# Batch 0 in a new order: beacons by a casting DMA, one transposed piece per score group, 96-token transposes for pairs 4 to 11

## The chip, the cores and the metric

The kernel runs on one core of a Trainium2 chip. The metric is the device time of one execution in microseconds (us), lower is better. A comparison uses runs of both kernels made on the same chip in the same rounds. A run more than 1.5% above the fastest run of its kernel is called slow, and only fast runs enter a ratio. PE is the matrix engine, PEld its weight loads, DVE the vector engine, ACT the scalar engine, POOL the GpSimd engine, SP (SyncE) an engine that here only issues DMA. SPq and POOLq are the issuing sides of these engines. kT<-k_dram and the like name what is written and what is read; st is a staging buffer, sc the scores, p a pair that was cast to bf16.

## The reference

There are 8 batches of 8 heads, 576 tokens, 16 beacons and a head size of 64. Beacons are extra keys and values that stand ahead of the tokens. A feed-forward layer with a maximum of three products follows.

```python
scores = scale * np.matmul(q, concat([beacon_k, k]).T)      # causal over the tokens only
a = softmax(scores)
x = np.matmul(a, concat([beacon_v, v]))                     # -> [4608 tokens, 512]
h = np.maximum(np.maximum(x @ w1, x @ w2), x @ w3)          # 512 -> 768
out = h @ w_out                                             # 768 -> 512
```

## The kernel before

The 32 pairs of heads (four in each batch) are worked through in order. For each pair the kernel needs q and k transposed (qT and kT, three buffers of each), computes scores in four groups on PE, takes exp on ACT, and later multiplies with v on PE (PV). The feed-forward units fill PE in between. PE transposes pairs 0 to 11 (batches 0 to 2) itself. For pairs 12 to 31, POOL casts the staged data to bf16, SyncE stores it to DRAM, and a transposing DMA fetches it back into qT and kT.

Loads, stores, transposing fetches and the output stores are nearly all issued by SyncE, which takes them in order. How loads are issued:

```python
st_pool = ctx.enter_context(tc.tile_pool(name="st", bufs=9))      # staging buffers for q/k pairs and v pieces
...
loads = [L(load_pair, 0, nc.scalar), L(load_beacons, 0, B_PE, bk32_0)]   # the beacons use no staging buffer
loads += [L(load_pair, 1, nc.scalar)] + load_pairs(2, 4) + load_v_pieces(0)
loads += load_pairs(4, 8) + load_v_pieces(1)
loads += load_pairs(8, 12) + load_v_pieces(2) + [L(load_beacons, B_PE, B, bk32)]
for b in range(B_PE, B):
    loads += load_pairs(b * PPB, (b + 1) * PPB) + load_v_pieces(b)

def next_load(n=1):                   # issue the next n of the list
    for _ in range(n):
        if loads:
            loads.pop(0)()

def C(fn, *a):                        # a cast frees a staging buffer, then one more load is issued
    def run():
        fn(*a)
        next_load()
    return run

def start():
    keep_busy(14)
    next_load(10)                     # 10 entries = 9 staged loads + the beacons
    ...
```

Nine buffers and nine staged loads: at first, each later load is issued just after the cast that frees its own buffer. Here are the fetch and the store of pairs 12 to 31, and their places in the program, where `p` is the first pair of batch `b`:

```python
def store_pair(p):                    # nc.sync.dma_start, twice (L276)
def fetch_pair(p):                    # nc.sync.dma_start_transpose into qT (L283) and kT (L284)
...
    at_step(p + i - 4, 0, C(cast_pair, p + i, by_pool, by_pool))
    at_step(p + i - 3, 0, L(store_pair, p + i))
    at_step(p + i - 2, 1, L(fetch_pair, p + i))
```

Pairs 0 to 11 are loaded as 128 rows of nine tokens each (packets of 2304 bytes), transposed in 36 tiles of 64, and DVE copies both results out of PSUM. The line numbers in the profile are those of the kernel concerned. The score matmul is L361 before and L381 after; kT's two DVE copies are L309 (16 beacon columns) and L310 (576 token columns), after the change L329 and L330; the v loads are L207 and L214; the q and k loads of 96 rows are L166 and L173; the v casts on POOL are L223 and L230; the fetches are L283 and L284, after the change L291 and L292, and the stores L276, after the change L284.

The softmax here doesn't subtract the row's maximum and nothing guards it: scores larger than these inputs give would overflow.

## Time and profile before

| | before |
|---|---|
| median of 3 runs | 308.89 us (308.16 to 312.95) |
| span of the profiled execution | 304.3 us |
| PE busy | 285.4 us, 94% of the span |
| DMA, share of busy time up to 86 us (about 1 is full; the records add up to a little more) | 0.86 to 1.11 |
| first exp of pairs 0, 5, 12, 31 | 10.76, 37.84, 93.66, 238.82 us |

The profile's page of the kernel before, cut to lines of its parts 2 and 4: the span in 40 slices, each digit a busy share in tenths (PEclk is the clock granted to PE), and then the shares of the chain of work that ended last.

```profile
PE   7698789899899999999999999999999999999994
PEclk9999999999999999999999999999999999999999
DMA  7999999799999999999999999688214001103003
...
PE 86%; DVE 6%; issue 2%; ACT 2%; DMA 1%; SPq 0%; POOL 0%; POOLq 0%; DVEq 0%
```

After the first dozen slices PE is full until the last one. The table by windows of the kernel before, cut to four rows, says the same; its columns are the window, its length, the busy time of PE, PEld, DVE, ACT and POOL with the number of instructions, the granted clock, the DMA share and GB/s.

```profile
10.00:37.00 27.00, 24.09 (x502) 13.34 (x502) 16.87 (x45) 18.53 (x27) 12.98 (x21) 1.00 1.11 258
37.00:86.00 49.00, 44.27 (x689) 22.35 (x700) 32.54 (x65) 24.19 (x36) 27.55 (x56) 1.00 1.03 247
86.00:120.00 34.00, 33.63 (x471) 17.08 (x476) 19.33 (x37) 18.67 (x28) 17.96 (x36) 1.00 1.01 235
120.00:240.00 120.00, 119.00 (x1566) 64.56 (x1580) 71.50 (x136) 63.24 (x94) 57.44 (x115) 1.00 0.83 175
```

From 86 to 240 us PE is busy 99% of the time. PE idles earlier: in batch 0 and in pairs 5 to 11. The clock column needs care here: the trace holds no clock record before 24.06 us, and a matmul of 256 columns takes 0.40 us ahead of that and 0.28 us after it, so the 1.00 of the first window is only the lack of a record.

The waits of the kernel before (engine and line, the releaser, then us in total, times, longest us), cut to two lines, one for what the scores wait for and one for SyncE.

```profile
PE sc L361 <- DVE kT L310: 5.6, 6, 2.8
...
SPq L166 <- POOL v_sb L223: 1.6, 1, 1.6
```

The scores wait for DVE's copies and, once, 0.6 us for ACT; no score waits for a fetched kT. This is what SyncE does around the first fetch, that of pair 12 (timeline of SyncE before: start, duration, engine, line, operation, tiles, count). Its scores start on PE at 93.17 us.

```profile
83.68 4.21 SPq L207 DMA_DIRECT2D st<-in_v_dram  x3
87.99 1.78 SPq L283 DMA_TRANSPOSE qT<-q_dram  x1
89.83 1.24 SPq L284 DMA_TRANSPOSE kT<-k_dram  x1
...
92.21 1.18 SPq L207 DMA_DIRECT2D st<-in_v_dram  x2
```

The fetch is issued behind three v loads, and two more v loads follow it. The trace gives 92.49 us as the landing of kT, so the fetch has 0.7 us to spare. Nothing in the views of waits shows how little that is.

### The profile page before, as it was taken

The numbers are of one execution on the slowest core, as the hardware profiler recorded it, in microseconds if no ns is written. First come the engines' busy times: TensorE is split into PE (matmuls) and PEld (weight loads), VectorE is DVE, ScalarE is ACT, GpSimd is POOL, SyncE is SP. The second block draws the span as 40 slices with busy tenths as digits, with TensorE's granted clock in tenths as the row PEclk, the third lists the DMA queues.
The fourth block names the chain that finished last, engine by engine and source line by source line (L and its number), as shares of the span: only waits on it lengthen the run. The fifth ranks groups of instructions, "written<-read, shape, count | busy, mean of one in ns | idle before, by whom it ended". The sixth has DMA issues, their size and how long they took to land.

```text
span 304.3 us, 8877 instructions
## 1 busy us (share of the span) xinstructions
PE 285.4 (94%) x3673; PEld 147.7 (49%) x3710; DVE 177.3 (58%) x343; ACT 139.2 (46%) x208; POOL 122.3 (40%) x243
## 2 busy tenths in 40 slices
PE   7698789899899999999999999999999999999994
PEld 4254544445454545454545777545454554444441
DVE  1695557774766465646564656465646574284472
ACT  3467754355436354635463546354635431401300
POOL 3580673465744554455445544654243210000000
PEclk9999999999999999999999999999999999999999
DMA  7999999799999999999999999688214001103003
GB/s 251 254 317 238 248 289 211 174 243 227 309 242 187 235 287 234 184 239 295 212 195 242 281 200 208 124 182 129 55 54 125 2 2 69 72 1 137 3 0 138
DMA packets 87976, 53.96 MB, mean 177 GB/s; under 512 B 67200, under 2 KB 79488, under 8 KB 87936
## 3 DMA queue, kind: packets, MB, share of 16 engines
q1 hardware_dynamic: 86000, 49.66, 69.2%
q0 software_dynamic: 1648, 3.15, 5.5%
q8 instruction: 29, 0.48, 0.7%
q10 hardware_dynamic: 288, 0.59, 0.6%
q14 instruction: 11, 0.09, 0.1%
HBM read 35.13 MB, written 15.42 MB: 166 GB/s over the span
## 4 chain that ended last, share of the span: by engine, by line
PE 86%; DVE 6%; issue 2%; ACT 2%; DMA 1%; SPq 0%; POOL 0%; POOLq 0%; DVEq 0%
PE fps L469 41%; PE pv L423 12%; PE fps L486 12%; PE sc L361 10%; PE sc L469 5%; PE sc L486 2%; DVE qT L301 1%; DVE kT L310 1%; DMA bk<-in_beacon_k_dram 1%; PE fps L330 1%; DVE xT L446 1%; DVE hT L479 1%; ACT at_sb L370 1%; DVE kT L309 1%; PE fps L293 1%
## 5 line engine op out<-in xcount | busy, mean ns | idle before, releaser
L370 ACT ACTIVATE at_sb<-sc 128x992 bf16<-128x992 f32 (+3 forms) x128 | 103.9, 860 | 106.7 <-PE sc L361 104.2
L469 PE MATMUL fps<-xT,w_sb 128*128 128x512 bf16 (+1 forms) x622 | 136.6, 355 | 1.9 <-issue 0.8
L469 PEld LDWEIGHTS <-w_sb 128*128 128x128 bf16 x720 | 65.7, 97 | 71.0 <-issue 13.4
L386 POOL TENSOR_SCALAR_AFFINE_SELECT at_sb<-at_sb 128x256 bf16<-128x256 bf16 (+2 forms) x140 | 51.1, 384 | 114.5 <-ACT at_sb L370 114.5
L479 DVE TENSOR_TENSOR hT<-hT,fps 128x512 bf16<-128x512 bf16 x96 | 65.6, 685 | 39.0 <-PE fps L469 39.0
L361 PE MATMUL sc<-qT,kT 64*128 64x288 bf16 (+4 forms) x384 | 37.7, 294 | 6.3 <-DVE kT L310 5.6
L486 PE MATMUL fps<-w_out_sb,hT 128*128 128x512 bf16 x172 | 40.6, 379 | 1.0 <-issue 0.8
L477 DVE CAST hT<-fps 128x512 bf16<-128x512 f32 x42 | 28.9, 689 | 20.8 <-PE fps L469 20.8
L494 DVE COPY y<-fps 128x512 f32<-128x512 f32 x30 | 20.7, 688 | 27.7 <-PE fps L486 27.7
L486 PEld LDWEIGHTS <-hT 128*128 128x128 bf16 x216 | 20.4, 98 | 25.2 <-DVE hT L479 1.3
L446 DVE TENSOR_TENSOR xT<-pv,recip 128x288 bf16<-128x288 f32 (+2 forms) x96 | 28.1, 348 | 6.4 <-ACT recip L443 3.8
L180 POOL CAST p<-st 96x768 bf16<-96x768 f32 x40 | 31.8, 822 | 0.0
L361 PEld LDWEIGHTS <-kT 64*128 64x128 bf16 x384 | 13.6, 95 | 33.6 <-issue 22.9
L423 PE MATMUL pv<-at_sb,v_sb 128*32 128x96 bf16 (+8 forms) x1408 | 29.4, 230 | 0.0
L423 PEld LDWEIGHTS <-v_sb 128*32 128x32 bf16 (+1 forms) x1408 | 24.4, 97 | 2.2 <-issue 0.9
L223 POOL CAST v_sb<-st 128x1536 bf16<-128x1536 f32 (+2 forms) x24 | 21.1, 894 | 2.8 <-DMA st<-in_v_dram 2.8
L423 PE MATMUL pv<-at_sb,ones 128*32 128x288 bf16 (+4 forms) x512 | 17.5, 258 | 1.6 <-DVE xT L446 1.5
L469 PE MATMUL sc<-xT,w_sb 128*128 128x512 bf16 x71 | 18.3, 380 | 0.1
L441 ACT ACTIVATE lnd<-pv 128x288 f32<-128x288 f32 x32 | 13.2, 413 | 8.0 <-PE pv L423 7.3
L479 DVE TENSOR_TENSOR hT<-hT,sc 128x512 bf16<-128x512 bf16 x12 | 8.2, 687 | 12.5 <-PE sc L469 6.8
L423 PEld LDWEIGHTS <-ones 128*32 128x32 bf16 (+1 forms) x512 | 10.9, 96 | 8.1 <-DVE xT L446 2.6
L443 ACT ACTIVATE recip<-lnd 128x288 f32<-128x288 f32 x32 | 14.2, 443 | 1.0
(38 smaller groups left out, 108.2 us busy)
## 6 DMA issues: line engine op xcount, KB each, us to landing
st<-in_q_dram SPq DMA_DIRECT2D x32, 288.0 KB, 5.0
out_dram<-y SPq DMA_DIRECT2D x36, 256.0 KB, 3.6
st<-in_k_dram SPq DMA_DIRECT2D x30, 288.0 KB, 5.3
st<-in_v_dram SPq DMA_DIRECT2D x24, 256.0 KB, 5.6
q_dram<-p SPq DMA_DIRECT2D x20, 144.0 KB, 2.2
k_dram<-p SPq DMA_DIRECT2D x20, 144.0 KB, 2.3
w_sb<-in_moe_w_dram POOLq DMA_DIRECT2D x6, 384.0 KB, 8.4
st<-in_v_dram SPq DMA_DIRECT2D x8, 224.0 KB, 5.6
```

What stands on the lines that cost most here:

```text
L180: cast(t16.rearrange("p r h d -> p h r d"), st[0:QP, i * NQ2 : (i + 1) * NQ2].rearrange("p (h r d) -> p h r d", h=2, r=QR),)
L223: cast(v_sb[0:n, t:t1].rearrange("p t h d -> p (t h d)"), st[0:n, (t - t_lo) * H * D : (t1 - t_lo) * H * D],)
L361: nc.tensor.matmul(ps[:, e, off : off + q1 - q0], kT[hs, 128 * t : 128 * t + 128], qT[hs, q0:q1], start=True, stop=True, tile_position=(64 ...
L370: nc.scalar.activation(out=both_heads(p, gi), in_=ps[:, :, 0 : g_width[gi]], func=AF.Exp, scale=scale)
L386: nc.gpsimd.affine_select(out=view, in_=view, compare_op=ALU.is_ge, fill=0.0, base=x0, pattern=[[0, 2], [1, hi - lo]], channel_multiplier=-1,)
L423: nc.tensor.matmul(ps[32 * j : 32 * j + 32, bank, lo + q0 - qa : lo + qb - qa], lhsT, at_view(PPQ * quad + j // 2, t, j % 2, q0, qb), star ...
L446: nc.vector.tensor_mul(xT[:, 2 * g + part - 1, c0 + ca : c0 + cb], ps[:, bank, lo : lo + cb - ca], recip[:, ca:cb],)
L469: nc.tensor.matmul(ps[:, o0 : o0 + n], w_in[i][:, ct, 128 * ft : 128 * (ft + 1)], xT[:, ct, x0 : x0 + n], start=(ct == 0), stop=(ct == n_c ...
L477: (by_act if alone[0] else by_dve)(hT[:, ft, :], ps)
L479: nc.vector.tensor_max(hT[:, ft, :], hT[:, ft, :], ps)
L486: nc.tensor.matmul(ps, hT[:, ft, 128 * tt : 128 * (tt + 1)], w_out_sb[:, ft, :], start=(ft == 0), stop=(ft == n_ft - 1),)
L494: nc.vector.tensor_copy(y, ps)
```

## The change

The intent is an earlier start and fewer waits in batch 0. The beacons come by a casting DMA from POOL, so that POOL has no cast to make. The transposes of batch 0 are spread, one piece behind each score group, instead of a whole pair behind the first. Pairs 4 to 11 are loaded as 96 rows of six tokens (packets of 1536 bytes) and turned by 12 transposes of 96 tokens; from pair 6 on ACT copies q out beside DVE, which copies k. The first weight load moves from step (1,1) to (0,3), and two feed-forward units move forward to step (4,3). The diff, cut to its core:

```diff
+    P_NINE = 4
...
+    for b in range(B_PE):
+        nc.gpsimd.dma_start(
+            out=bk16_0[Nb * b : Nb * (b + 1)], in_=beacon_k[b].rearrange("h n d -> n h d")
+        )
...
-            if b < B_PE:
+            if p < P_NINE:                       # 128 rows of 9 tokens, else 96 rows of 6
...
-    loads = [L(load_pair, 0, nc.scalar), L(load_beacons, 0, B_PE, bk32_0)]
-    loads += [L(load_pair, 1, nc.scalar)] + load_pairs(2, 4) + load_v_pieces(0)
-    loads += load_pairs(4, 8) + load_v_pieces(1)
-    loads += load_pairs(8, 12) + load_v_pieces(2) + [L(load_beacons, B_PE, B, bk32)]
-    for b in range(B_PE, B):
+    loads = [L(load_pair, 0, nc.scalar), L(load_pair, 1, nc.scalar)] + load_pairs(2, 4)
+    loads += load_v_pieces(0)
+    loads += load_pairs(4, 6) + load_v_pieces(1) + load_pairs(6, 8)
+    for b in range(2, B):
+        if b == B_PE:
+            loads.append(L(load_beacons, B_PE, B, bk32))
         loads += load_pairs(b * PPB, (b + 1) * PPB) + load_v_pieces(b)
...
     def start():
-        keep_busy(14)
+        keep_busy(13)
         next_load(10)
...
-        by_pool(bk16_0, bk32_0)
...
     def turn(p, i, ps):
         src = stage.pop(("pair16", p, i))
+        if p >= P_NINE:
+            for r in range(QR):
+                nc.tensor.transpose(ps[:, r * QP : (r + 1) * QP], ..., ident[0:QP, 0:QP])
+            return
...
-        copy(kT[:, 0:Nb], bT[:, pi, Nb * b : Nb * (b + 1)])
+        if p > 0:
+            copy(kT[:, 0:Nb], bT[:, pi, Nb * b : Nb * (b + 1)])
...
-    at_step(1, 1, L(load_w, 0, 0, d_ff))
+    at_step(0, 3, L(load_w, 0, 0, d_ff))
...
+    fine_at = {
+        (0, 0): [L(turn_apart, 1, 0)],
+        (0, 1): [L(turn_apart, 1, 1)],
+        ...
+        (2, 2): [L(turn_apart, 4, 0)],
+        (2, 3): [L(turn_apart, 4, 1)],
+        ...
+    }
...
-                    turn_pair(nxt, False)
+                    turn_pair(p + 1, by_act)
```

## The prediction

> **What bounds the kernel now.** The chain of waits is 86% PE. The table by windows splits the run: from about 86 us on PE is busy 98-99%, so only time saved before that counts, and it then counts in full. Before, there are three kinds of loss.
> (a) Start: the first scores run at 10.11 us. The chain shows why: the beacon DMA lands at 6.2, POOL casts it (0.61), PE turns it, ACT copies it, then DVE copies kT 1.69 + 0.67 us.
> (b) Batch 0 (10.1 to 37.0, where pair 5's scores start): 20 score groups whose exps cost ACT 17.3 us; PE runs slow until 24.06 us, where the trace's first full-clock record stands (a 256-column matmul takes 0.40 us before it, 0.28 after).
> (c) Pairs 5 to 10 (37 to 86 us): PE idle about 5 us in the windows, mostly 0.6-0.7 us a pair waiting for DVE's qT (0.76) and then kT (0.16 + 0.74) drain.
>
> **What the change does.**
> Start: the POOL cast and the wait of kT for the beacons vanish; first scores near 7.6 us, 2.5 earlier.
> Batch 0: the same turns, but 18 transposes between score groups; fewer keep-busy matmuls; PV a little later; two FFN units (8 matmuls of 0.215 = 1.7 us) pulled forward.
> Later turns: 12 transposes of 96 columns for 36 tiles of 64, about the same PE time (0.76 us now). ACT drains q (about 0.64) beside DVE's k, which takes some 0.5 us a pair off the wait, five or six times: about 2.5-3 us.
>
> **What gives part of it back: the DMA queue.** DMA is saturated from 6 to 36 us (share 1.0 in the windows). The weight load w0 now is issued right after pair 3's casts, at about 11.4 instead of 15.5 us, and its first packet should flow 3.6 us later as before (15.5 to 19.1), thus near 15, when the second part of v (landed 17.3 now) and pairs 4 and 5 (17.8-20.1) are still under way. The Trainium skill ("DMA: Bandwidth & Descriptors", Queues, rings and completion order) says that an engine goes round-robin between queues, packet by packet; the trace agrees: while weights flow (packets of 247 ns) beside v (256-byte packets, 18 ns), the weights' queue takes 0.93 of the DMA and v 0.15 (26 to 28 us). So v's second part should slip to about 20-21 us and pair 4 to 22-23, while pair 4's first turn stands in PE's order at group (2,2), otherwise reached near 20. PE stalls there for 2-3 us, and the start's gain is lost. From there ACT's exps and four normalisations pace the rest: pair 5's scores at 36-37.7 us, but with two FFN units done.
>
> **Sum.** Pair 5: -0.7 to +1; units +1.7; later waits +2.5 to 3; and, if pair 4 is not late, up to 3 more. About 5.7 us off 308.9.
>
> Predicted **303.2 us**, 299 to 307.5. Faster by over 2%: 0.43; within: 0.53; slower: 0.04.
>
> **What would show it.** First scores at 7.4-8 us; POOL's cast of pair 4 waiting for v or pair 4 data at 20-23 us and PE idle then; pair 5's scores near 36; waits of scores for kT in pairs 5-10 down from 0.65 to below 0.15 us; windows after 86 us unchanged in length; busy PE time about 1-2 us less.
>
> **What would make it wrong.** If w0 does not push v and pair 4 back, batch 0 ends at 33-34 and the time is about 300. If the slow PE clock lasts longer (fewer keep-busy matmuls, an idle stretch), the gain shrinks to 2-3 us. If the 96-column turns cost 1 us or more each, or ACT's added copies delay exps, (c) is lost. Run-to-run spread (308.2 to 313.0) is as large as half the effect.

## The result, and the profile after

| | before | after |
|---|---|---|
| median us (lowest to highest), 4 runs of each in the same rounds | 309.00 (308.16 to 312.95) | 329.52 (326.88 to 330.18) |
| span of the profiled execution, us | 304.3 | 327.2 |
| first exp of pair 5 | 37.84 | 37.70 |
| pair 9 | 68.67 | 64.32 |
| pair 11 | 86.52 | 86.65 |
| pair 12 | 93.66 | 100.11 |
| pair 16 | 124.09 | 137.12 |
| pair 24 | 185.05 | 208.89 |
| pair 31 | 238.82 | 262.65 |

The change makes the kernel slower: ratio 1.0658, 95% interval 1.0583 to 1.0733. All ratios here are the mean time of one kernel's fast runs over that of the other's fast runs of the same rounds, so they are not quite the ratio of the medians that stand beside them.

The table of first exps, read from the trace, is the main reading: up to pair 9 the new kernel is 4.35 us ahead, at pair 11 the lead is gone, and from pair 12 to pair 24 it falls 23.8 us behind. From there on both run alike. The page of the kernel after, the same lines:

```profile
PE   5868999986948996999699985999999999999995
PEclk9587999997996998999989997999999999999999
DMA  8999999899999399967999579826732300301103
...
PE 78%; DMA 8%; DVE 5%; SPq 4%; issue 2%; ACT 1%; POOL 0%; DVEq 0%
```

PE has holes up to slice 25, and after several of them PEclk has a dip as well. SyncE and DMA now stand in the chain, with 12% between them. The table by windows of the kernel after:

```profile
10.00:37.00 27.00, 22.23 (x441) 13.06 (x439) 17.37 (x48) 19.63 (x28) 13.17 (x18) 0.77 1.15 225
37.00:86.00 49.00, 43.11 (x545) 21.72 (x548) 32.45 (x55) 26.54 (x40) 29.68 (x58) 0.97 1.04 238
86.00:120.00 34.00, 27.31 (x357) 13.76 (x362) 14.44 (x28) 13.72 (x21) 13.49 (x28) 0.90 0.90 203
120.00:240.00 120.00, 108.49 (x1394) 59.92 (x1406) 62.88 (x119) 54.97 (x83) 54.07 (x106) 0.96 0.82 182
```

Between 86 and 240 us PE is idle 18.2 us, where it had been idle 1.4. The waits of the kernel after, cut to four lines:

```profile
PE sc L381 <- DMA kT<-k_dram: 16.8, 4, 6.0
PE sc L381 <- DVE kT L330: 5.0, 5, 3.6
PE fps L300 <- POOL p L187: 2.2, 1, 2.2
...
SPq L173 <- POOL v_sb L230: 14.3, 3, 6.1
```

Four score groups wait 16.8 us for a fetched kT; before there was no such wait. One waits 3.6 us for a DVE copy. SyncE, in turn, waits 14.3 us with a load in hand for a staging buffer that POOL's v casts free; before it was 1.6. The timeline of PE in the kernel after, cut to those four score groups (the bracket is the idle time ahead and the releaser):

```profile
99.41 0.90 PE L381 MATMUL sc<-qT,kT 64*128 64x288 bf16 x8 [6.04 <-DMA kT<-k_dram]
...
127.94 0.54 PE L381 MATMUL sc<-qT,kT 64*128 64x288 bf16 x8 [2.87 <-DMA kT<-k_dram]
...
163.16 0.90 PE L381 MATMUL sc<-qT,kT 64*128 64x288 bf16 x8 [3.15 <-DMA kT<-k_dram]
...
199.69 0.57 PE L381 MATMUL sc<-qT,kT 64*128 64x288 bf16 x8 [4.70 <-DMA kT<-k_dram]
```

They are the scores of pairs 12, 15, 19 and 23: one in each batch from 3 to 5, and two in the first of these. The timeline of SyncE in the kernel after, around the first of them and then into the second:

```profile
87.08 3.13 SPq L214 DMA_DIRECT2D st<-in_v_dram  x1
...
91.68 0.43 SPq L284 DMA_DIRECT2D q_dram<-p  x1
92.15 1.56 SPq L284 DMA_DIRECT2D k_dram<-p  x1
93.81 1.10 SPq L214 DMA_DIRECT2D st<-in_v_dram  x2
95.02 1.54 SPq L291 DMA_TRANSPOSE qT<-q_dram  x1
96.61 1.25 SPq L292 DMA_TRANSPOSE kT<-k_dram  x1
...
105.96 1.22 SPq L292 DMA_TRANSPOSE kT<-k_dram  x1
113.39 0.31 SPq L173 DMA_DIRECT2D st<-in_q_dram  x1
```

The fetch of pair 12 now stands behind all the v loads and behind two stores. It is issued 6.8 us later than before (96.61 against 89.83 for kT) and lands at 99.37 us. And between 107.2 and 113.4 us SyncE issues nothing at all: it holds the q load of pair 22, whose buffer is freed by the v cast that POOL ends at 113.36 us. The table by windows shows the DMA engines resting at a share of 0.02 from 109 to 114 us, while later fetches wait behind that load.

The clock records of the kernel after, in the trace: full speed from 29.40 to 77.19 us, then half speed at 77.19 to 80.60, 97.67 to 104.50, 128.39 to 131.80, 162.52 to 165.94 and 200.07 to 203.48. Each of these starts around the end of one of PE's long waits. The Trainium skill ("TensorE: Matmul & The Clock Gate", Part 1: The HAM clock gate) says that the clock is judged in free-running windows of 3413 ns and falls to one half after an idle one. The lengths agree: the half-speed records last 3413 ns and 6827 ns. But the window ahead of a drop need not be wholly idle: in the 3.41 us before these five drops PE was busy 0.80, 0.00, 0.54, 0.89 and 0.38 us, while every window after 30 us that full speed followed held 1.7 us or more. So a missed fetch costs its wait and then a slow stretch: after its 6.04 us of waiting, pair 12 took 9.76 us to pair 13, against 7.68 before.

The wait of 3.6 us for DVE is of another kind. The timelines of DVE and of POOL in the kernel after, around pair 10's copy of 16 beacon columns (128x16, SBUF to SBUF):

```profile
72.04 3.65 DVE L329 COPY kT<-bT 128x16 bf16<-128x16 bf16 x1
```

```profile
70.68 1.60 POOL L187 CAST p<-st 96x768 bf16<-96x768 f32 x2
72.23 0.77 POOL L406 TENSOR_SCALAR_AFFINE_SELECT at_sb<-at_sb 128x256 bf16<-128x256 bf16 x2
72.94 1.60 POOL L187 CAST p<-st 96x768 bf16<-96x768 f32 x2
74.47 1.18 POOL L230 CAST v_sb<-st 128x512 bf16<-128x512 f32 x2
```

The eight POOL instructions follow each other without a gap from 70.68 to 75.65 us. The copy, which takes 0.16 us when POOL is idle (pair 2, 15.42 us), starts inside this run, and ends 0.03 us after it.

### The profile page after: what moved, and what is told of

The parts are those of the page before. It is cut to its first block, busy times and chain, and to the rows that moved or that the text cites. A ratio compares the mean times of both kernels' runs of the same rounds, so it can differ in the third digit from the quotient of the medians.

```text
span 327.2 us, 8462 instructions
## 1 busy us (share of the span) xinstructions
PE 289.3 (88%) x3470; PEld 150.2 (46%) x3501; DVE 176.5 (54%) x336; ACT 141.9 (43%) x215; POOL 126.3 (39%) x245
## 3 DMA queue, kind: packets, MB, share of 16 engines
HBM read 35.13 MB, written 15.42 MB: 154 GB/s over the span
## 4 chain that ended last, share of the span: by engine, by line
PE 78%; DMA 8%; DVE 5%; SPq 4%; issue 2%; ACT 1%; POOL 0%; DVEq 0%
PE fps L493 38%; PE pv L447 12%; PE fps L510 12%; PE sc L381 8%; PE sc L493 5%; DMA kT<-k_dram 4%; DMA st<-in_k_dram 3%; PE sc L510 2%; SPq L214 2%; DMA st<-in_q_dram 2%; DVE kT L329 2%; DVE kT L330 1%; SPq L291 1%; DVE hT L503 1%; DVE xT L470 1%
## 5 line engine op out<-in xcount | busy, mean ns | idle before, releaser
L493 PE MATMUL fps<-xT,w_sb 128*128 128x512 bf16 (+1 forms) x627 | 139.5, 360 | 2.3 <-issue 1.0
L493 PEld LDWEIGHTS <-w_sb 128*128 128x128 bf16 x720 | 66.6, 99 | 73.3 <-issue 17.3
L381 PE MATMUL sc<-qT,kT 64*128 64x288 bf16 (+4 forms) x384 | 38.0, 299 | 22.9 <-DMA kT<-k_dram 16.8
L187 POOL CAST p<-st 96x768 bf16<-96x768 f32 x56 | 45.0, 828 | 7.4 <-issue 4.9
L447 PE MATMUL pv<-at_sb,v_sb 128*32 128x192 bf16 (+4 forms) x1352 | 32.1, 247 | 0.0
L510 PEld LDWEIGHTS <-hT 128*128 128x128 bf16 x216 | 20.5, 98 | 25.0 <-DVE hT L503 1.3
L470 DVE TENSOR_TENSOR xT<-pv,recip 128x288 bf16<-128x288 f32 (+2 forms) x93 | 27.3, 348 | 7.6 <-ACT recip L467 7.6
L447 PEld LDWEIGHTS <-v_sb 128*32 128x32 bf16 (+1 forms) x1408 | 27.4, 105 | 2.4 <-issue 0.4
L447 PE MATMUL pv<-at_sb,ones 128*32 128x288 bf16 (+4 forms) x492 | 19.6, 279 | 0.4 <-DVE at_sb L404 0.4
L493 PE MATMUL sc<-xT,w_sb 128*128 128x512 bf16 x71 | 18.3, 379 | 0.1
L447 PEld LDWEIGHTS <-ones 128*32 128x32 bf16 (+1 forms) x512 | 11.7, 102 | 9.0 <-issue 6.5
```

The source lines that it names most:

```text
L187: cast(t16.rearrange("p r h d -> p h r d"), st[0:QP, i * NQ2 : (i + 1) * NQ2].rearrange("p (h r d) -> p h r d", h=2, r=QR),)
L381: nc.tensor.matmul(ps[:, e, off : off + q1 - q0], kT[hs, 128 * t : 128 * t + 128], qT[hs, q0:q1], start=True, stop=True, tile_position=(64 ...
L447: nc.tensor.matmul(ps[bank][32 * j : 32 * j + 32, lo + q0 - qa : lo + qb - qa], lhsT, at_view(PPQ * quad + j // 2, t, j % 2, q0, qb), star ...
L470: nc.vector.tensor_mul(xT[:, 2 * g + part - 1, c0 + ca : c0 + cb], ps[bank][:, lo : lo + cb - ca], recip[:, ca:cb],)
L493: nc.tensor.matmul(ps[:, o0 : o0 + n], w_in[i][:, ct, 128 * ft : 128 * (ft + 1)], xT[:, ct, x0 : x0 + n], start=(ct == 0), stop=(ct == n_c ...
L510: nc.tensor.matmul(ps, hT[:, ft, 128 * tt : 128 * (tt + 1)], w_out_sb[:, ft, :], start=(ft == 0), stop=(ft == n_ft - 1),)
```

## The experiments

Two candidate causes followed from the two traces, and both are silent consequences of the diff. The first theory is the **load place**. The list of loads lost the beacons' entry while `next_load(10)` stayed. So ten staged loads are now issued at the start where there were nine, for nine buffers, and every later load stands one place earlier on SyncE: from pair 12's load on it comes right behind the cast that frees its buffer, where one more cast had lain between, and the stores and fetches behind the load wait with it. The rival is the **96-row form** of pairs 4 to 11 (smaller packets, slower loads). A third, smaller suspect is DVE's copy blocked by POOL. In the text "staged loads at the start" counts loads that need a buffer; it is the number that the experiments turn.

### e1_load9: one staged load less, all else as after

```diff
-        next_load(10)
+        next_load(9)
```

> The kernel after, with 9 instead of 10 loads issued at the start, which puts SyncE's whole later order (loads, stores, transposing fetches) back to that of before; nothing else changes. Theory Q (queue order: the beacons' load left the list, so every later load stands one place earlier on SyncE's in-order queue, ahead of stores and fetches, and waits there for a staging buffer): the four waits of scores for the fetched kT (16.8 us together) fall under 2 us, the half-clock stretches after 70 us go, and the time is 300 to 308 us. Rival L (the 96-row loads of pairs 4 to 11 take more DMA time, so fetches come late): still 320 us or more, kT waits over 10 us.

Measured: 311.64 us, ratio to before 1.0074 (1.0014 to 1.0135). One number of the kernel gives back 17.9 of the 20.5 us. From the waits of this kernel:

```profile
PE sc L381 <- DMA kT<-k_dram: 5.5, 3, 4.4
PE sc L381 <- DVE kT L330: 5.0, 5, 3.6
...
SPq L173 <- POOL v_sb L230: 8.7, 4, 3.7
```

Of the fetch waits, 4.4 us stay, at pair 12; the ones at pairs 15, 19 and 23 are gone, and 0.73 and 0.40 us stand at pairs 16 and 24. The DVE wait is untouched. The expectation was too good: it had named 300 to 308 us, fetch waits under 2 us and no half clock, but half speed stays at 75.9 to 79.3 and 96.3 to 103.2 us, and SyncE still waits 8.7 us for v casts.

### e2_before_load11: the kernel before with one staged load more

```diff
-        next_load(10)
+        next_load(11)
```

> The kernel before, with 11 instead of 10 loads at the start: SyncE's later order becomes that of after, everything else is before. Theory Q: the loss comes into the kernel before by this alone: 318 to 330 us, scores waiting for fetched kT 8 us or more, half-clock stretches after 90 us. Rival L, and a rival that blames batch 0's new order: no change, 306 to 312 us.

Measured: 326.60 us, ratio 1.0538 (1.0445 to 1.0630). The kernel before, made slower by this one number, shows the marks of the kernel after:

```profile
PE sc L361 <- DMA kT<-k_dram: 13.4, 4, 4.1
...
SPq L166 <- POOL v_sb L223: 12.6, 3, 4.4
```

Half-clock records stand at 97.4, 124.7, 162.3 and 196.4 us, again by pairs 12, 15, 19 and 23. So the load place is enough for most of the loss without any other part of the change.

### e3_nine_rows: the rival alone

```diff
-    P_NINE = 4
+    P_NINE = 12
```

Pairs 4 to 11 are loaded and transposed in the old form, with ACT still copying q out.

> The kernel after, with pairs 4 to 11 loaded and turned in the old 9-row form (128 rows of 2304 bytes, 36 transposes of 64). Theory Q: still slow, 318 to 330 us, since SyncE's order is that of after. Rival L: the DMA gets its 4 us back by 60 us, and the time is 302 to 310 us.

Measured: 321.68 us (317.75 to 322.99); two of the four runs count as slow, and no ratio is given. Waits for fetched kT are 13.7 us, four times. The rival explains a part, about 8 us of medians (10 if only the two fast runs, 317.75 and 320.78 us, count), and not the greater one.

### e4_load9_nine: both repairs

Both edits above, nine staged loads and `P_NINE = 12`.

> Both: 9 loads at the start and the old 9-row form for pairs 4 to 11. Theories Q and L both: 300 to 307 us. Against e1 this shows what the 96-column turns and loads cost or gain once the queue order is back: by Q within 2 us either way.

Measured: 306.18 us, ratio 0.9891 (0.9828 to 0.9953). With both side effects away, the reordering of batch 0 is a gain, of about 3 us. One fetch wait of 3.5 us remains, and the half clock at 91.7 to 98.5 us with it. The expectation had put the 96-row form at 2 us or less; e1 minus e4 is 5.5 us.

One reason why the 96-row form costs time is seen in the table by windows for 34 to 40 us, when both kernels load almost nothing but pairs. The first line is of the kernel after, the second of e4:

```profile
34.00:40.00 6.00, 5.48 (x43) 2.46 (x42) 4.55 (x10) 3.65 (x7) 4.84 (x10) 1.00 1.09 263
```

```profile
34.00:40.00 6.00, 4.38 (x60) 2.23 (x55) 5.48 (x9) 2.94 (x4) 5.04 (x11) 1.00 1.04 391
```

The DMA engines are full in both (1.09 and 1.04), but move 263 against 391 GB/s. In these windows a packet of 1536 bytes took 101 ns on average and one of 2304 bytes 97 ns: the smaller packet took as long and brought a third less. Pairs 4 to 11 are 4.72 MB, which is 17.9 us at the one rate and 12.1 us at the other. This estimate of 5.9 us is close to what the form costs at nine staged loads (311.64 - 306.18 = 5.5 us). The fetch of pair 12's kT is issued at 94.53 us in e1 and at 90.12 us in e4. The form also makes each of POOL's casts longer (0.82 us instead of 0.66, two a pair for eight pairs, thus some 2.6 us); no experiment parts the packets from the casts, so the share of each is not shown.

### e5_load8_nine: one place later still

```diff
-    P_NINE = 4
+    P_NINE = 12
...
-        next_load(10)
+        next_load(8)
```

> e4 (old 9-row form for pairs 4 to 11) with 8 loads at the start instead of 9: the loads move one place further back on SyncE's queue, so the fetch of pair 12 stands ahead of batch 3's v loads. Theory Q: pair 12's wait for its fetched kT (3.5 us in e4) falls under 1 us, the half-clock stretch near 92 us goes, pair 12's first exp runs at 89 to 91 us (93.6 in e4), and the time is 2 to 5 us under e4, 301 to 304 us. Rival (pair 12's wait is set by DMA bandwidth, not by the place in the queue): wait still 3 us or more, same time as e4.

Measured: 301.59 us (before in these rounds 308.56), ratio 0.979 (0.9713 to 0.9866). This beats both kernels. A line of the waits and one of the windows of e5:

```profile
PE sc L381 <- DMA kT<-k_dram: 1.5, 2, 1.3
```

```profile
120.00:240.00 120.00, 120.00 (x1602) 64.81 (x1602) 70.41 (x134) 62.23 (x95) 57.05 (x115) 1.00 0.81 175
```

PE is full from 120 to 240 us, the clock never drops there, and SyncE's waits for a v cast are at most 0.4 us. The fetch of pair 12 is issued at 83.68 and 85.02 us, ahead of the v loads. By now a load is issued two casts after the one that frees its buffer, and it does not hold the queue; at one cast after it, SyncE had waited 1.6 us (before) and 8.7 us (e1) for v casts. The last wait, 1.3 us at pair 12, is a little longer than expected (under 1).

### e9_load8_rows96, and the control e11_before_load9

The first is the kernel after with `next_load(8)` only. The second is the kernel before with `next_load(9)`, thus eight staged loads.

> The kernel after with 8 loads at the start instead of 10, nothing else: the smallest repair of the queue. Theory Q: no wait over 1.5 us of scores for the fetched kT; what is left against e5 is the 96-row form, above all pair 10's stall behind GpSimd's casts (about 3.6 us) and the half clock after it: 303.5 to 308 us. Rival (the 96-row form keeps its fetch waits whatever the queue): 309 us or more.

> Control: the kernel before with 9 loads at the start instead of 10, so with the loads one place later on SyncE's queue. By theory Q the kernel before has no wait for a fetched kT to lose, so no gain: 306 to 311 us, within 0.7% of before. If it gains 2% or more, e5's gain is the queue's and not the change's.

Measured: e9 307.99 us, ratio 0.9967 (0.9924 to 1.0010); e11 307.52 us, ratio 0.9963 (0.9921 to 1.0004). The kernel before gains nothing that can be told from zero, so the gain of e5 is not the load place alone. The medians of nine kernels now form a table, in us, from four sets of rounds in which the kernel before had medians of 308.56 to 309.32:

| staged loads at the start | 10 | 9 | 8 |
|---|---|---|---|
| 96-row form (after, e1, e9) | 329.5 | 311.6 | 308.0 |
| 128-row form (e3, e4, e5) | 321.7 | 306.2 | 301.6 |
| order of before, 128-row form (e2, before, e11) | 326.6 | 309.3 | 307.5 |

In the first two rows each step is of like size: ten to nine is worth 15.5 to 17.9 us, nine to eight 3.7 to 4.6, the form 5.5 to 7.8. (With e3's fast runs alone, mean 319.3 us, its first step is about 13 us and the form costs about 10 at ten loads.) The third row shows what the two traces alone did not: at an equal load place the reordering gains 3.1 and 5.9 us in the 128-row form (nine and eight loads), while the whole diff, with the 96-row form, still costs 0.5 us (not told from zero) to 2.9 us. In e9 one wait of 5.9 us remains, at pair 12, and none at pairs 15, 19 and 23; the expectation had allowed 1.5 us, and had looked for pair 10's stall behind POOL, which fell to 0.3 us here. The form makes the loads late once, before pair 12; the load place makes them late again in each batch.

### e6_plain_beacons: give back the early start

e5, with the beacons by a plain load on SyncE and a DVE cast (nine entries, thus eight staged loads).

```diff
-    for b in range(B_PE):
-        nc.gpsimd.dma_start(
-            out=bk16_0[Nb * b : Nb * (b + 1)], in_=beacon_k[b].rearrange("h n d -> n h d")
-        )
...
+    loads = [L(load_pair, 0, nc.scalar), L(load_beacons, 0, B_PE, bk32_0), L(load_pair, 1, nc.scalar)] + ...
...
+        next_load(9)
...
+        by_dve(bk16_0, bk32_0)
```

> e5 with the beacons of batches 0 to 2 loaded by plain DMA on SyncE's queue right after pair 0's q, as before, and cast by VectorE; the rest as e5. If the casting DMA on the software queue is what makes them late (landed 8.5 to 8.9 us in after and e4, 6.2 in before), they land near 6.2, the first exp runs at 7.7 to 8.3 us instead of about 9.7. What follows for the whole: by the prediction's step (pair 4's loads set when the fine stage ends) pair 5's exp moves by less than 0.7 us and the time is within 1 us of e5; by the rival (each us at the start counts) the time falls by 1.5 to 2 us.

Measured: 303.63 us, ratio 0.9846 (0.9774 to 0.9919), some 2 us slower than e5 in the same rounds; neither side of the expectation had this. The first exp came at 8.04 us rather than 10.31 (beacons landed at 6.25 us instead of 8.64), but pair 5's came at 39.21 rather than 36.61. PE waited 3.4 us for pair 4's cast (its data landed at 21.56 and 22.37 us), and its clock was half from 16.3 to 26.6 us and from 40 to 43.6 us. A start 2.3 us earlier ended batch 0 later. The trace shows that pair 4's late arrival is the wait that ends last in this stage; how much of the loss is the slow clock and how much the late data was not tested apart.

### e7_late_w0: take the weight load out of v's way

```diff
-    at_step(0, 3, L(load_w, 0, 0, d_ff))
     at_step(1, 0, C(cast_v, 0, 0, by_pool))
+    at_step(1, 0, L(load_w, 0, 0, d_ff))
```

on top of e5.

> e5 with the first weight load issued after the first v cast, as before, instead of right after pair 3's casts. By the prediction: v's last piece lands near 17 us instead of 20, pair 4 near 19 instead of 21.6, PE's stall for pair 4 (2.3 us in e4) goes, pair 5's first exp comes 1.5 to 3 us earlier than in e5 and the time falls by 1 to 3 us. Rival (the stage is paced by ACT and the slow clock anyway): less than 0.5 us.

Measured: 303.03 us, ratio 0.9857 (0.9750 to 0.9964). The mechanism is as the prediction had it: v's last piece landed at 16.9 instead of 19.8 us, and pair 4 at 17.5 and 18.3 us instead of after 20.3. But pair 5's first exp stayed (36.90 against 36.61), where 1.5 to 3 us were expected. The time saved was lost further on: POOL's run of work from batch 1's v casts to pair 6's casts now fell on DVE's kT copy, which took 2.12 us at 33.65 us. (In e12, where ACT makes that copy, pair 5's first exp comes at 35.06.)

### e8_act_beacon_copy: DVE's blocked copy

On top of e1, ACT makes the copy of the 16 beacon columns from pair 6 on.

```diff
-            copy(kT[:, 0:Nb], bT[:, pi, Nb * b : Nb * (b + 1)])
+            (by_act if p > PPB + 1 else copy)(kT[:, 0:Nb], bT[:, pi, Nb * b : Nb * (b + 1)])
```

> e1 (96-row form, 9 loads) with the 16 beacon columns of kT copied by ScalarE instead of VectorE for pairs 6 to 11; nothing else. Theory S (that VectorE copy, SBUF to SBUF, waits until GpSimd's run of casts ends: 3.65 us in e1 at 71.7 us, 0.16 when GpSimd is idle): the wait of pair 10's scores falls from 3.6 us to under 0.5, the half-clock stretch at 76 us goes, pair 10's exp runs at 72.5 to 73.5 us (76.8 in e1); pair 12's wait for its fetch grows by as much as is not hidden there, so the time is 0 to 4 us under e1. Rival (pair 10's data come late by the 96-row DMA): pair 10 still at 76 us or later.

Measured: 310.98 us, ratio 1.0091 (1.0016 to 1.0165), against 1.0074 for e1: no gain. These lines are from the waits of e8:

```profile
PE sc L381 <- DMA kT<-k_dram: 9.6, 2, 9.4
...
PE sc L381 <- DVE kT L330: 0.5, 3, 0.2
```

The wait for DVE is gone, from 3.6 us to 0.2 at the longest, and pair 11 starts 5.2 us earlier than in e1 (81.00 against 86.22). But the wait for pair 12's fetch has grown by 5.0 us, and pair 12 starts at 97.80 us against 98.01. A wait that lies ahead of a longer one costs nothing as long as the longer one stands. In the kernel after, the blocked copy is real and large, and with the half clock after it, it explains why the lead of pair 9 is gone at pair 11; by e8 its repair alone would have moved the time little, though that was tried on e1 only and not on the kernel after itself.

### e10_all_repairs and e12_late_w0_act

e12 is e7 with ACT's copy from pair 5 on. e10 is e12 with e6's plain beacons as well. Both have eight staged loads.

> e5 (8 loads, 9-row form) with plain beacons, the late first weight load, and ScalarE copying the 16 beacon columns for pairs 5 to 11. If e6 lost because its early start ran into late v and pair 4, and e7 because pair 5's copy (2.1 us) sat behind GpSimd's casts, then together: first exp near 8 us, no stall over 1 us before pair 4's turn, pair 5's first exp at 34 to 36 us (36.6 in e5), 299 to 301 us. Rival (batch 0 is paced by what arrives by DMA, w1 and batch 1's v included): pair 5 not before 36.3, time as e5 within 1 us.

> e7 (late first weight load) with ScalarE copying the 16 beacon columns for pairs 5 to 11. By theory S pair 5's scores no longer wait for that copy (2.12 us in e7), pair 5's first exp comes at 35 to 36 us (36.9 in e7) and the time is 0.8 to 2 us under e7, 301 to 302.3 us. Rival: no change beyond 0.5 us.

Measured: e10 306.36 us, ratio 0.992 (0.9878 to 0.9962); e12 304.76 us (300.93 to 306.46, the last a slow run), ratio 0.9828 (0.9750 to 0.9905). Both reached pair 5 earlier than e5 (35.59 and 35.06 us against 36.61), and both lost it at pair 12: they wait for fetched kT 5.3 us (e10, the longest 4.0) and 3.5 us (e12), where e5 waited 1.5. They had been expected at 299 to 301 and at 301 to 302.3 us. They reached pair 11 0.2 and 1.0 us ahead of e5 (80.99 and 80.16 against 81.21), but the kT of pair 12 landed at 91.69 and 90.36 us, while in e5 its scores ran at 89.19.

### e13_load7_nine and e14_load7_late_w0_act: one place later again

e13 is e5 with `next_load(7)`; e14 is e12 with `next_load(7)`.

> e5 with 7 loads at the start instead of 8: one load fewer ahead of pair 12's stores and fetch on the DMA queues. If pair 12's last wait (1.3 us in e5) and the larger ones of e10 and e12 come from loads standing ahead of the fetch, the wait is gone (under 0.5 us) and the time is 0.5 to 1.5 us under e5, about 300.5 us. If bandwidth sets it, the wait and the time stay; if loads now come too late, a wait of GpSimd for its loads appears and the time rises above 303 us.

> e12 (late first weight load, ScalarE copying the beacon columns) with 7 loads. Loads ahead of the fetch: pair 12's wait (3.5 us in e12) falls under 1 us, no half-clock stretch near 91 us, 299.5 to 301.5 us, the best of all. Bandwidth: the wait stays at 3 us or more, 303 us or more.

Measured: e13 301.16 us, ratio 0.976 (0.9711 to 0.9808); e14 300.68 us, ratio 0.9768 (0.9701 to 0.9835). From the waits of e14:

```profile
PE sc L381 <- DMA kT<-k_dram: 1.5, 1, 1.5
```

Its wait at pair 12 fell from 3.5 us (e12) to 1.5, and half speed no longer occurs between 30 us and the end. This one number moved kT's landing from 90.36 to 87.84 us, so in e12 too, loads ahead of the fetch held it; but 1.5 us stay where under 1 was expected, and in e13 2.1 us in three waits where under 0.5 was. The timeline of SyncE in e14 at pair 12's fetch (as in e5 and e12, batch 4's v loads come after it):

```profile
81.31 0.34 SPq L173 DMA_DIRECT2D st<-in_k_dram  x1
82.37 1.64 SPq L291 DMA_TRANSPOSE qT<-q_dram  x1
84.12 1.20 SPq L292 DMA_TRANSPOSE kT<-k_dram  x1
```

e14 has the lowest median of all kernels, 8.0 us below the kernel before in its rounds. The intervals of e5, e13 and e14 overlap, so which of the three is best stays open. All three lie surely below the kernel before; whether by more than 2% is not decided by their intervals.

## Why the prediction was wrong

The prediction was 303.2 us with 4% for slower by over 2%. Measured was 329.52 us.

**The step that failed** stands in its first paragraph: "from about 86 us on PE is busy 98-99%, so only time saved before that counts, and it then counts in full", and again as "windows after 86 us unchanged in length". The reading of the profile was right: PE was busy 99% there. The inference from it was not. A stage where PE is full shows that nothing else was late in *that* kernel, not that nothing else can be. Pair 12's kT landed 0.7 us ahead of its use. The diff moved every load one place forward on the queue that carries the fetches, and the prediction never compared the order of SyncE's instructions, although that could be read before any run. Of the 20.5 us, the load place took 17.9 (after minus e1). That a single number, with all else alike, makes the kernel before nearly as slow (e2, 326.60 us) shows the cause.

**A second step was mis-sized**: "Later turns: 12 transposes of 96 columns for 36 tiles of 64, about the same PE time". For PE this was right (0.68 us against 0.76 at full clock). But the form of the loads came with it, and at a full DMA queue 1536-byte packets moved 263 GB/s against 391. The form as a whole cost 5.5 us (e1 minus e4). The prediction said that DMA is saturated up to 36 us, and did not ask what the new packets did to it.

**Put together**, in medians: -3.1 us for the reordering itself (e4 minus its kernel before, 306.18 - 309.32), +5.5 for the 96-row loads, +17.9 for the load place. The sum, unrounded, is +20.2, against +20.5 measured; this is no test, since differences along a chain of kernels must add up, and the 0.3 is the shift of the kernel before between rounds. Along the other chain (after, e3, e4) the form has 7.8 and the load place 15.5, with e3's slow runs in its median. The prediction of -5.7 compares with the -3.1, which still contains one wait of 3.5 us at pair 12; in e5, with 1.5 us of such waits, it is -7.0, or -5.9 against e11 with its equal load place. That this is near -5.7 confirms little: the prediction counted the 96-row turns, which e5 doesn't have, and its terms came out differently, as follows.

Point by point, the rest of the prediction:

- **First scores at 7.4 to 8 us: wrong.** They came at 9.88 us. The casting DMA took away POOL's cast but landed its three parts at 6.59, 7.97 and 8.85 us, where the plain load had landed at 6.2. Both were issued at about 1.3 us, but its first packet came at 5.27 us against 3.80, and its 384 packets (128 bytes in the record) took 3.2 us, among larger ones of other queues, against 1.5. That the second part is the Trainium skill's round-robin between queues ("DMA: Bandwidth & Descriptors", Queues, rings and completion order) fits the trace, but it is not shown, and it does not explain the late first packet; e6's earlier landing (6.25 us) tests neither apart, for e6 changed the issuing engine as well.
- **The weight load pushes back v and pair 4: right.** It was issued at 10.99 us; v's last piece landed at 20.41 us and pair 4 at 21.60 and 22.79 us (predicted 20 to 21, and 22 to 23). PE then waited 2.2 us for pair 4's cast. e7 confirms the cause and shows that its removal alone gains nothing.
- **Pair 5's scores at 36 to 37.7 us with two units done: right, in part by luck.** They came at 37.28 us, with the 2.2 us stall as predicted, but the gain of 2.5 us at the start that it was to use up had not been there (first scores 0.24 us earlier).
- **Later waits shorter by 2.5 to 3 us: right up to pair 9.** At pair 9 the kernel is 4.35 us ahead, of which two units moved forward are 1.7. In e5, pairs 5 to 11 take 44.6 us where they took 48.7. **Wrong at pair 10,** where POOL blocked DVE's copy for 3.65 us; from pair 5 on, waits of scores for DVE's kT came to 5.0 us, against 2.9. The others fell to 0.16 to 0.47 us, not below 0.15.
- **Busy PE time about 1 to 2 us less: wrong.** It rose from 285.4 to 289.3 us; matmuls at half clock take longer (0.40 against 0.28 us for 256 columns) and count as busy.
- **What would make it wrong** named the slow clock, but as a loss of start-up work. It came instead with each missed fetch: each of the four waits, 2.9 to 6.0 us long, came with a stretch of half speed and so cost a second time.

What stays open: the last 1.5 to 2.1 us of waiting for pair 12 or later fetches in e5, e13 and e14; how the 96-row form's cost parts into packets and casts; why an earlier start (e6, e10) ends batch 0 or batch 2 no earlier in this order of work, whether by the clock or by the data; and which of e5, e13 and e14 is best.

## What to carry to other kernels

When a diff adds or removes an entry of a shared list of issues, count again how many loads are issued ahead and how many buffers there are, and compare the order of the DMA queue entry by entry: a load whose buffer is not free yet holds every store and fetch behind it. A stage in which the matrix engine is 99% busy is safe only by the slack of its tightest transfer, so read that slack (landing time against first use) before saying that a stage won't change. And when one wait is repaired, look for the later wait that may take up all of the gain.

## What the Trainium skill lacked or had wrong

- "SBUF — State Buffer", Who interferes with whom, says of the port pair that DVE and GpSimd share that the lock is held for one whole instruction and that the loser fully blocks. The runs show the loser blocked for longer than one instruction: a DVE copy of 16 columns (0.16 us alone) ended 0.03 us after the last of a run of back-to-back POOL instructions and took 3.65 us, with parts or all of seven POOL instructions of 0.4 to 0.8 us inside it. That the lock went from one POOL instruction to the next ahead of the waiting copy is what these times suggest. It does not always last to the end of a run: at 84.10 us in the same trace the copy took 1.36 us and ended 0.03 us after the second of three such instructions. ACT making the copy (e8) took 0.23 us.
- "DMA: Bandwidth & Descriptors", Bandwidth, gives its measured rates for 128 partitions. At a full DMA queue, loads of 96 rows in packets of 1536 bytes moved 263 GB/s and loads of 128 rows in packets of 2304 bytes 391 GB/s. A packet took 101 and 97 ns. The two differ in rows, in packet size and in the pattern of heads, and the runs don't tell these apart.
- The same page, Latency and other measured facts, gives about 1 us for the first byte of a DMA issued by GpSimd. With DMA saturated by another queue, the first packet of the casting weight loads came 3.6 us after issue (15.48 to 19.1 us in the kernel before) and 3.85 us (36.51 to 40.36 us); in the kernel after it was 2.4, 1.9 and 5.1 us.
- The same page, Anatomy of one DMA, puts a DMA's wait for a semaphore on the issuing sequencer, ahead of the issue; none of the pages read says what such a wait costs the DMA instructions behind it. Here SyncE issued nothing for 6.2 us (107.2 to 113.4 us), and the DMA engines' share was 0.02.
